# A causal convolution and a maxout feed-forward layer on one core: the second convolution bank is copied out behind the next relu, and the copy of the repacked block into the upper partitions is issued one block later, behind the x cast

## The chip, the cores and the metric

The kernel runs on one core of a Trainium2 chip. Its time is the device time of one execution in microseconds (us). Three runs of the kernel before took 529.06, 526.87 and 526.42 us; the median is 526.87 us. All data is drawn at random once and is the same in every run.

## The reference

```python
# x: 8 x 4160 x 192, weight: 8 heads x 7 taps; group = 192 / 8 = 24 channels a head
w   = softmax(weight, axis=-1)
out[b, s, h, :] = sum over k of w[h, k] * x_padded[b, s + k, h, :]    # 6 zero rows ahead of each sequence
y   = out.reshape(33280, 192)
h   = max(max(y @ w1, y @ w2), y @ w3)                               # 192 x 768 each
result = h @ w_out                                                   # 768 x 192, float32
```

The kernel uses max(a, b, c) = max(a - c, b - c, 0) + c: it multiplies y by w1 - w3 and by w2 - w3 (both in `wd`), takes relu of the first product and the maximum with the second, multiplies by w_out, and adds y @ (w3 @ w_out), whose small matrix (`m16`) it computes once at the start.

## The kernel before

**Blocks.** The 33280 tokens are cut into 65 blocks of 512 tokens. Work on a block goes through these stages, each on its own engine:

- `load_x` (SP's queue) reads the block's rows of x into a float32 tile `xf`; `cast_x` (POOL, L133) turns them into float16 (`x16`).
- `conv` (TensorE, L222) computes the convolution as 40 matmuls against a banded matrix. Heads 0 to 3 go to one PSUM bank, G0, and heads 4 to 7 to a second one, G1. ScalarE (L231) copies G0 and then G1 into the tile `ys`.
- `repack` moves `ys` to the tile `yd`, where the 192 channels lie as 3 x 64 rows, by ten small DMAs on SP's queue (L259, "pieces" below). It runs once for a group of two blocks (the first two groups have one block each). One more DMA, on POOL's queue (L260), copies partitions 0 to 63 of `yd` to partitions 64 to 127; it is called the duplicate below. It waits until all pieces have landed, and POOL does nothing else while it waits at its head.
- `l1` (L273) computes one sixth of the 768 hidden rows, here called a sub-tile: six matmuls, three into a bank of `lp` (from partitions 0 to 63 of `yd` and `wd`) and three into a bank of `lq` (from partitions 64 to 127). The two kinds use different halves of the TensorE's rows and run side by side. Then ScalarE writes r = relu(lp) (L277), and VectorE writes h = max(r, lq) (L278). `lp` and `lq` have two banks each, so a sub-tile takes the banks of the one before the last: its `lq` matmuls wait until the max of two sub-tiles earlier is done.
- `st2` (L309) multiplies h by w_out and y by `m16` into banks `po`, again with one stream on each half of the rows: 30 pairs of matmuls a block, cut into five equal slices. ScalarE copies one half of `po` (L313), VectorE adds the other (L314), and `store` (POOL's queue, L323 and L328) writes the block to memory.

**Banks.** G0, G1 and the four `po` tiles of a block rotate through four PSUM banks, so the second pair of `po` tiles of a block takes the banks that G0 and G1 of the same turn had.

**Order.** Each engine runs its instructions in the order in which the code issues them; the order is written out by hand. The main loop turns once a block. Turn t issues: the load of block t+6; the cast of block t+5; sub-tile 0 of block t; the convolution of block t+4 with both bank copies; the repack with the duplicate, where t+4 ends a group; then sub-tiles 1 to 5 of block t, each followed by one slice of `st2` of block t-1; and the store of block t-1. The last four turns (blocks 61 to 64) have no convolution left.

**Queues.** A DMA on SP's queue waits until the DMA eight places ahead of it has landed. POOL's stream holds the casts, the duplicates and the stores in one line.

Of the kernel before, what the change touches and what calls it, by code (L numbers as in the profile page):

```python
# [14 lines left out]
P = 128  # L15
# [6 lines left out]
NBLK = 512  # L22
# [4 lines left out]
def kernel(  # L27
# [12 lines left out]
    nc = tc.nc  # L40
# [6 lines left out]
    NJ = DFF // P  # L47
# [20 lines left out]
    NB = len(blocks)  # L68
    blkN = [sum(sg[2] for sg in blk) for blk in blocks]
# [29 lines left out]
    groups = [[0], [1]] + [list(range(t, min(t + 2, NB))) for t in range(2, NB, 2)]  # L99
    group_of = {t: (g, k) for g, ts in enumerate(groups) for k, t in enumerate(ts)}  # L100
    AHEAD = 4
# [3 lines left out]
    def load_x(t):  # L105
        if not 0 <= t < NB:
            return
        chunks = chunks_of[t]
        xf = xfp.tile([P, NQMAX, D], FP32, tag="xf", name=f"xf_{t}")
        parts = []  # L110
        i, n = 0, len(chunks)
        while i < n:
            k = i
            while (k + 1 < n and chunks[k][3] == P and chunks[k + 1][3] == P
                   and chunks[k + 1][1] == chunks[k][1]
                   and chunks[k + 1][2] - chunks[k][2] == CHK):
                k += 1
            (_, b0, row0, rlen0, _, _, _) = chunks[i]
            cnt = k - i + 1
            src = bass.AP(tensor=x.tensor, offset=(b0 * SEQ + row0) * D,  # L120
                          ap=[[D, rlen0], [CHK * D, cnt], [1, D]])
            nc.sync.dma_start(out=xf[0:rlen0, i:k + 1, :], in_=src)
            parts.append((rlen0, i, k + 1))
            i = k + 1
        xin[t] = [xf, None, parts]

    def cast_x(t):
        if not 0 <= t < NB:
            return
        xf, _, parts = xin[t]  # L130
        x16 = x16p.tile([P, NQMAX, D], FP16, tag="x16", name=f"x16_{t}")
        for (rl, q0, q1) in parts:
            nc.gpsimd.tensor_copy(out=x16[0:rl, q0:q1, :], in_=xf[0:rl, q0:q1, :])  # L133
        xin[t][1] = x16
# [19 lines left out]
    for k in range(KW):  # L154
        nc.vector.tensor_mul(out=taps[:, KW - 1 - k, :], in0=wexp[:, k, :], in1=wrec[:])
    nc.scalar.dma_start(
        out=bass.AP(tensor=Rd[:].tensor, offset=Rd[:].offset,
                    ap=[[BW + NHEAD, P], [1, KW * NHEAD]]),
        in_=taps[:].rearrange("p k h -> p (k h)"))
# [5 lines left out]
    HALF, NC = 64, D // 64  # L165
# [25 lines left out]
    def make_m():  # L191
        nc.scalar.copy(out=wo[:], in_=wos[:])
        for g in range(NJ // 2):
            ps = psq.tile([P, 2, D], FP32, tag="q", name=f"pt{g}")
            for k in range(2):
                js = slice(P * (2 * g + k), P * (2 * g + k + 1))
                for c in range(NC):
                    nc.tensor.transpose(ps[:, k, HALF * c:HALF * (c + 1)], w3s[0:HALF, c, js],
                                        ident[0:HALF, 0:HALF])
            nc.vector.tensor_copy(out=w3t[:, 2 * g:2 * g + 2, 0:D], in_=ps[:])  # L200
            nc.vector.tensor_copy(out=w3t[:, 2 * g:2 * g + 2, D:2 * P], in_=ps[:, :, P:D])
        for i in range(2):
            ps = psp.tile([P, D], FP32, tag="p", name=f"pm{i}")
            for j in range(NJ):
                nc.tensor.matmul(ps[:], lhsT=w3t[:, j, P * i:P * (i + 1)], rhs=wos[:, j, :],  # L205
                                 start=(j == 0), stop=(j == NJ - 1))
            nc.vector.tensor_copy(out=m16[:, i, :], in_=ps[:])


    slots, dense, hs, outs, halves = {}, {}, {}, {}, {}  # L210

    def conv(t):
        if t >= NB:
            return
        N = blkN[t]
        G = [psw.tile([P, NBLK], FP32, tag="w", name=f"G{i}_{t}") for i in range(2)]
        x16 = xin[t][1]
        for (q, b, row_lo, rlen, lo, hi, cc) in chunks_of[t]:
            for h in range(NHEAD):
                g = h % 4  # L220
                cb = GRP * h if h < NHEAD - 1 else GRP * h - 8
                nc.tensor.matmul(  # L222
                    G[h // 4][32 * g:32 * g + 32, lo:hi],
                    lhsT=x16[0:rlen, q, cb:cb + 32],
                    rhs=band[0:rlen, h, cc:cc + hi - lo],
                    start=True, stop=True, tile_position=(0, 32 * g))
        g, k = group_of[t]
        if k == 0:
            slots[g] = ysp.tile([P, 2, 2 * NBLK], FP16, tag="ys", name=f"ys_{g}")
        for i in range(2):  # L230
            nc.scalar.copy(out=slots[g][:, i, NBLK * k:NBLK * k + N], in_=G[i][:, 0:N])  # L231
        xin.pop(t)

    pieces = []
    for h in range(NHEAD):
# [7 lines left out]
    def repack(t):  # L243


        if t >= NB or t != groups[group_of[t][0]][-1]:
            return
        g, k = group_of[t]
        yd = dense[g] = ydp.tile([P, NC, 2 * NBLK], FP16, tag="yd", name=f"yd_{g}")
        w = slice(0, NBLK * (k + 1))  # L250
        if g == 0:
            qs = (nc.sync, nc.scalar, nc.gpsimd)
            todo = [(lo, p) for p in pieces for lo in (0, HALF)]
            for n, (lo, (half, s0, c, r0, rows)) in enumerate(todo):
                qs[n % 3].dma_start(out=yd[lo + r0:lo + r0 + rows, c, w],  # L255
                                    in_=slots[g][s0:s0 + rows, half, w])
            return
        for (half, s0, c, r0, rows) in pieces:
            nc.sync.dma_start(out=yd[r0:r0 + rows, c, w], in_=slots[g][s0:s0 + rows, half, w])  # L259
        nc.gpsimd.dma_start(out=yd[HALF:P, :, w], in_=yd[0:HALF, :, w])  # L260

    def l1(t, j):

# [13 lines left out]
        nc.scalar.activation(out=r[:, 0:N], in_=ps[0][:, 0:N], func=AF.Relu)  # L277
        nc.vector.tensor_max(out=hs[t][:, j, 0:N], in0=r[:, 0:N], in1=ps[1][:, 0:N])  # L278

    NU = 5  # L280

    def st2(t, u):

        if t < 0:
            return
        g, k = group_of[t]
        hT, y = hs[t], dense[g]
        if u == 0:  # L290
            todo = [[], []]
            for s in range(4):
                tok = slice(NBLK * k + P * s, NBLK * k + P * (s + 1))
                for i in range(2):
                    row = slice(HALF * i, HALF * (i + 1))
                    mm = [(y[row, i, tok], m16[row, 0, :])]
                    if s % 2 == i:
                        mm.append((y[row, 2, tok], m16[row, 1, :]))
                    mm += [(hT[row, j, P * s:P * (s + 1)], wo[row, j, :]) for j in range(NJ)]
                    todo[i] += [(s, n == 0, n == len(mm) - 1, m) for n, m in enumerate(mm)]  # L300
            halves[t] = (todo, {})
        todo, ps = halves[t]
        n = len(todo[0])
        for e in range(n * u // NU, n * (u + 1) // NU):
            for i in range(2):
                s, first, last, (a, b) = todo[i][e]
                if (s // 2, i) not in ps:
                    ps[s // 2, i] = psw.tile([P, 2, D], FP32, tag="w", name=f"po{i}_{t}_{s}")
                nc.tensor.matmul(ps[s // 2, i][:, s % 2, :], lhsT=a, rhs=b, start=first, stop=last)  # L309
            s, _, last, _ = todo[1][e]  # L310
            if last and s % 2 == 1:
                a = tp.tile([P, 2, D], FP32, tag="a", name=f"a_{t}_{s}")
                nc.scalar.copy(out=a[:], in_=ps[s // 2, 0][:])  # L313
                nc.vector.tensor_add(out=outs[t][:, s - 1:s + 1, :], in0=a[:], in1=ps[s // 2, 1][:])  # L314
# [16 lines left out]
    assert all(n == NBLK for n in blkN)  # L331
    for t in range(AHEAD):
        conv(t)
        repack(t)
        if t + 3 <= AHEAD + 1:
            load_x(t + 3)
        if t + 3 <= AHEAD:
            cast_x(t + 3)
        if t == 1:
            make_m()  # L340
    for t in range(NB):
        load_x(t + AHEAD + 2)
        cast_x(t + AHEAD + 1)
        hs[t] = hp.tile([P, NJ, NBLK], FP16, tag="h", name=f"h_{t}")
        outs[t] = outp.tile([P, 4, D], FP32, tag="o", name=f"o_{t}")
        l1(t, 0)
        conv(t + AHEAD)
        repack(t + AHEAD)
        for j in range(1, NJ):
            l1(t, j)  # L350
            st2(t - 1, j - 1)
        store(t - 1)
    for u in range(NU):
        st2(NB - 1, u)
    store(NB - 1)
# [1 line left out]
_INS = ['x', 'weight', 'moe_w1', 'moe_w2', 'moe_w3', 'moe_w_out']  # L357
# [26 lines left out]
```

## Time and profile before

| | us |
|---|---|
| Median of the runs | 526.87 (526.42 to 529.06) |
| The profiled execution's own time | 529.13 |
| Its span, from the first to the last instruction | 527.4 |
| TensorE (PE) busy | 481.8, 91% of the span |
| ScalarE (ACT) busy | 356.7, 68% |
| VectorE (DVE) busy | 336.6, 64% |
| POOL busy | 143.1, 27% |

The profile is of one execution. Times in it are microseconds from the span's start, and those of a single instruction in groups are nanoseconds. A timeline row gives an instruction's start, its length, its engine and line, the tile that it writes and those that it reads, how many were merged, and in brackets the idle time of the engine just before it and what ended this. A row of the view of waits gives an engine's line, what it waited for, the total in us, how many times, and the longest. PE's matmuls are pipelined and their ends are modelled, so the start of one to the start of the next says more than a length does.

### The profile page before, as it was taken

What the parts mean: (1) busy time and instruction counts of PE and PEld (TensorE: products, weight loads), DVE (VectorE), ACT (ScalarE), POOL (GpSimd) and SP (SyncE); (2) the same over time, 40 slices, a digit from 0 to 9 for tenths busy, and PEclk for the clock granted to TensorE, in tenths of its full rate; (3) what the DMA queues carried; (4) which work ended last, traced back from release to release, by engine and by line L of the source; (5) the groups of instructions that cost most, each with busy time, mean ns of one, the idle gap of its engine ahead of it and who ended that gap; (6) DMA issues with size and microseconds to landing.
All of it is one profiled execution on the core that took longest, in us unless ns stands there. A gap on an engine that the chain in (4) does not pass through costs nothing.

```text
span 527.4 us, 21248 instructions
## 1 busy us (share of the span) xinstructions
PE 481.8 (91%) x8906; PEld 359.9 (68%) x8906; DVE 336.6 (64%) x542; ACT 356.7 (68%) x654; POOL 143.1 (27%) x205
## 2 busy tenths in 40 slices
PE   0094999999999999999999999999999999999993
PEld 0082677777767777777777777777677777777773
DVE  1322677766667667676667776676666777676773
ACT  1133777777777777777777777777677777777662
POOL 1131133333331322333333222223333322322213
PEclk9997999999999999999999999999999999999998
DMA  7825566666655665666766656666666666654522
GB/s 178 203 78 129 141 189 190 193 189 192 194 141 161 179 175 155 192 192 193 188 185 176 163 165 166 183 168 185 187 191 188 186 171 171 177 140 128 140 70 61
DMA packets 65751, 87.72 MB, mean 166 GB/s; under 512 B 7592, under 2 KB 51304, under 8 KB 65656
## 3 DMA queue, kind: packets, MB, share of 16 engines
q1 hardware_dynamic: 54648, 47.36, 33.6%
q0 software_dynamic: 10224, 38.28, 25.3%
q8 instruction: 70, 1.15, 0.9%
q10 hardware_dynamic: 784, 0.72, 0.4%
q14 instruction: 25, 0.20, 0.1%
HBM read 34.93 MB, written 25.85 MB: 115 GB/s over the span
## 4 chain that ended last, share of the span: by engine, by line
PE 76%; DMA 8%; SPq 5%; POOL 3%; issue 3%; ACT 2%; ACTq 1%; DVE 1%; POOLq 0%
PE po L309 26%; PE lp L273 23%; PE lq L273 21%; PE G L222 6%; SPq L259 5%; DMA yd<-ys 3%; DMA Rd<-taps 2%; DMA xf<-in_x_dram 2%; POOL x L133 1%; DMA bandc<-Rd 1%; DMA Rd<-zero 1%; ACTq L255 1%; ACT r L277 1%; ACT ys L231 1%; DVE h L278 1%
## 5 line engine op out<-in xcount | busy, mean ns | idle before, releaser
L278 DVE TENSOR_TENSOR h<-r,lq 128x512 f16<-128x512 f16 x390 | 268.4, 688 | 153.7 <-ACT r L277 126.8
L273 PE MATMUL lq<-yd,wd 64*128 64x512 f16 x1170 | 316.2, 377 | 0.9 <-DVE h L278 0.7
L273 PE MATMUL lp<-yd,wd 64*128 64x512 f16 x1170 | 316.6, 378 | 0.0
L277 ACT ACTIVATE r<-lp 128x512 f16<-128x512 f32 x390 | 234.1, 600 | 109.8 <-PE lp L273 86.1
L309 PE MATMUL po<-wo,h 64*128 64x192 f16 x3120 | 230.3, 243 | 0.2 <-DVE h L278 0.2
L309 PEld LDWEIGHTS <-h 64*128 64x128 f16 x3120 | 189.8, 94 | 29.5 <-DVE h L278 0.4
L273 PEld LDWEIGHTS <-wd 64*128 64x128 f16 x2340 | 148.9, 94 | 51.5 <-issue 13.7
L309 PE MATMUL po<-m,yd 64*128 64x192 f16 x780 | 96.6, 243 | 0.0
L260 POOL DMA_DIRECT2D yd<-yd x33 | 18.1, 548 | 288.5 <-DMA xf<-in_x_dram 153.2
L231 ACT CAST ys<-G 128x512 f16<-128x512 f32 x130 | 69.8, 589 | 29.9 <-PE G L222 19.5
L222 PEld LDWEIGHTS <-x 128*32 128x32 f16 (+2 forms) x2624 | 37.0, 98 | 63.0 <-issue 38.8
L222 PE MATMUL G<-band,x 128*32 128x122 f16 (+3 forms) x2624 | 43.5, 212 | 36.2 <-DVE band L186 24.9
L133 POOL CAST x<-xf 128x960 f16<-128x960 f32 (+3 forms) x88 | 68.4, 794 | 30.0 <-DMA xf<-in_x_dram 29.2
L314 DVE TENSOR_TENSOR o<-a,po 128x384 f32<-128x384 f32 x130 | 71.2, 547 | 1.7 <-ACT a L313 1.7
L309 PEld LDWEIGHTS <-yd 64*128 64x128 f16 x780 | 58.2, 94 | 14.6
L323 POOL DMA_DIRECT2D out_dram<-o x64 | 49.1, 767 | 59.1 <-PE G L222 36.9
L313 ACT COPY a<-po 128x384 f32<-128x384 f32 x130 | 61.9, 476 | 2.0 <-PE po L309 1.9
L187 ACT COPY band<-bandc 128x536 f16<-128x536 f16 x1 | 2.6, 2569 | 17.2 <-DMA bandc<-Rd 17.2
L183 DVE TENSOR_TENSOR wd<-ws,w3s 128x768 f16<-128x768 f32 x3 | 2.7, 953 | 12.0 <-DMA w3s<-in_moe_w_dram 12.0
L205 PE MATMUL pm<-wos,w3t 128*128 128x192 f32 x24 | 6.9, 474 | 0.0
L205 PEld LDWEIGHTS pm<-wos,w3t 128*128 128x128 f32 x24 | 6.6, 298 | 0.1
L328 POOL DMA_DIRECT2D out_dram<-o x8 | 4.2, 537 | 0.8 <-DVE o L314 0.8
(20 smaller groups left out, 17.9 us busy)
## 6 DMA issues: line engine op xcount, KB each, us to landing
out_dram<-o POOLq DMA_DIRECT2D x64, 384.0 KB, 5.6
xf<-in_x_dram SPq DMA_DIRECT2D x48, 480.0 KB
yd<-yd POOLq DMA_DIRECT2D x31, 384.0 KB, 6.1
yd<-ys SPq DMA_DIRECT2D x186, 48.0 KB
xf<-in_x_dram SPq DMA_DIRECT2D x16, 384.0 KB
yd<-ys SPq DMA_DIRECT2D x62, 32.0 KB
ws<-in_moe_w_dram SPq DMA_DIRECT2D x2, 576.0 KB
w3s<-in_moe_w_dram SPq DMA_DIRECT2D x2, 576.0 KB
```

The source lines that it names most:

```text
L133: nc.gpsimd.tensor_copy(out=x16[0:rl, q0:q1, :], in_=xf[0:rl, q0:q1, :])
L222: nc.tensor.matmul(G[h // 4][32 * g:32 * g + 32, lo:hi], lhsT=x16[0:rlen, q, cb:cb + 32], rhs=band[0:rlen, h, cc:cc + hi - lo], start=True ...
L231: nc.scalar.copy(out=slots[g][:, i, NBLK * k:NBLK * k + N], in_=G[i][:, 0:N])
L259: nc.sync.dma_start(out=yd[r0:r0 + rows, c, w], in_=slots[g][s0:s0 + rows, half, w])
L260: nc.gpsimd.dma_start(out=yd[HALF:P, :, w], in_=yd[0:HALF, :, w])
L273: nc.tensor.matmul(ps[i][:, 0:N], lhsT=wd[row, c, P * j:P * (j + 1)], rhs=y[row, c, NBLK * k:NBLK * k + N], start=(c == 0), stop=(c == NC ...
L277: nc.scalar.activation(out=r[:, 0:N], in_=ps[0][:, 0:N], func=AF.Relu)
L278: nc.vector.tensor_max(out=hs[t][:, j, 0:N], in0=r[:, 0:N], in1=ps[1][:, 0:N])
L309: nc.tensor.matmul(ps[s // 2, i][:, s % 2, :], lhsT=a, rhs=b, start=first, stop=last)
L313: nc.scalar.copy(out=a[:], in_=ps[s // 2, 0][:])
L314: nc.vector.tensor_add(out=outs[t][:, s - 1:s + 1, :], in0=a[:], in1=ps[s // 2, 1][:])
L323: nc.gpsimd.dma_start(out=out[g0:g0 + n, :].rearrange("(s p) c -> p s c", p=P), in_=ob[:])
```

## The change

ScalarE's copy of the bank G1 is now issued behind the relu of sub-tile 1, and the repack follows it. The duplicate of a group becomes a function of its own, `double`, which is issued in the next turn of the loop, behind that turn's cast. In the four turns ahead of the loop it is issued behind the load and the cast of that turn. In the last four turns, which have no convolution, `st2` is cut into six slices instead of five, and its first slice comes directly behind sub-tile 0; the last block's `st2` is cut into six as well.

```diff
--- before.py
+++ after.py
@@ -207,7 +207,7 @@
             nc.vector.tensor_copy(out=m16[:, i, :], in_=ps[:])
 
 
-    slots, dense, hs, outs, halves = {}, {}, {}, {}, {}
+    slots, dense, hs, outs, halves, convs = {}, {}, {}, {}, {}, {}
 
     def conv(t):
         if t >= NB:
@@ -227,9 +227,15 @@
         g, k = group_of[t]
         if k == 0:
             slots[g] = ysp.tile([P, 2, 2 * NBLK], FP16, tag="ys", name=f"ys_{g}")
-        for i in range(2):
-            nc.scalar.copy(out=slots[g][:, i, NBLK * k:NBLK * k + N], in_=G[i][:, 0:N])
+        convs[t] = G
         xin.pop(t)
+
+    def evac(t, i):
+        if t >= NB:
+            return
+        g, k = group_of[t]
+        N = blkN[t]
+        nc.scalar.copy(out=slots[g][:, i, NBLK * k:NBLK * k + N], in_=convs[t][i][:, 0:N])
 
     pieces = []
     for h in range(NHEAD):
@@ -257,7 +263,13 @@
             return
         for (half, s0, c, r0, rows) in pieces:
             nc.sync.dma_start(out=yd[r0:r0 + rows, c, w], in_=slots[g][s0:s0 + rows, half, w])
-        nc.gpsimd.dma_start(out=yd[HALF:P, :, w], in_=yd[0:HALF, :, w])
+
+    def double(t):
+        if not 0 <= t < NB or t != groups[group_of[t][0]][-1] or group_of[t][0] == 0:
+            return
+        g, k = group_of[t]
+        w = slice(0, NBLK * (k + 1))
+        nc.gpsimd.dma_start(out=dense[g][HALF:P, :, w], in_=dense[g][0:HALF, :, w])
 
     def l1(t, j):
 
@@ -277,9 +289,7 @@
         nc.scalar.activation(out=r[:, 0:N], in_=ps[0][:, 0:N], func=AF.Relu)
         nc.vector.tensor_max(out=hs[t][:, j, 0:N], in0=r[:, 0:N], in1=ps[1][:, 0:N])
 
-    NU = 5
-
-    def st2(t, u):
+    def st2(t, u, NU):
 
 
 
@@ -331,27 +341,38 @@
     assert all(n == NBLK for n in blkN)
     for t in range(AHEAD):
         conv(t)
+        evac(t, 0)
+        evac(t, 1)
         repack(t)
         if t + 3 <= AHEAD + 1:
             load_x(t + 3)
         if t + 3 <= AHEAD:
             cast_x(t + 3)
+        double(t)
         if t == 1:
             make_m()
     for t in range(NB):
+        NU = NJ - 1 if t + AHEAD < NB else NJ
         load_x(t + AHEAD + 2)
         cast_x(t + AHEAD + 1)
+        if t > 0:
+            double(t + AHEAD - 1)
         hs[t] = hp.tile([P, NJ, NBLK], FP16, tag="h", name=f"h_{t}")
         outs[t] = outp.tile([P, 4, D], FP32, tag="o", name=f"o_{t}")
         l1(t, 0)
         conv(t + AHEAD)
-        repack(t + AHEAD)
+        evac(t + AHEAD, 0)
+        if NU == NJ:
+            st2(t - 1, 0, NU)
         for j in range(1, NJ):
             l1(t, j)
-            st2(t - 1, j - 1)
+            if j == 1:
+                evac(t + AHEAD, 1)
+                repack(t + AHEAD)
+            st2(t - 1, j - NJ + NU, NU)
         store(t - 1)
-    for u in range(NU):
-        st2(NB - 1, u)
+    for u in range(NJ):
+        st2(NB - 1, u, NJ)
     store(NB - 1)
 # ---- launch: one core; inputs and outputs as the reference has them ----
 _INS = ['x', 'weight', 'moe_w1', 'moe_w2', 'moe_w3', 'moe_w_out']
```

Two places show what moves. The first is ScalarE's order in turn 2 of the loop (r_1 is the relu of sub-tile 1, G_6_769 and G_6_770 are the banks G0 and G1 of block 6, a_1 is the first copy of `po`). Before:

```order
L231 CAST ys_811<-G_6_769 128x512
L231 CAST ys_811<-G_6_770 128x512
L277 ACTIVATE r_1_822<-lp_1_814 128x512
L277 ACTIVATE r_2_847<-lp_2_839 128x512
L277 ACTIVATE r_3_870<-lp_3_862 128x512
```

and now:

```order
L238 CAST ys_811<-G_6_769 128x512
L289 ACTIVATE r_1_821<-lp_1_813 128x512
L238 CAST ys_811<-G_6_770 128x512
L289 ACTIVATE r_2_847<-lp_2_839 128x512
L289 ACTIVATE r_3_870<-lp_3_862 128x512
```

The relu of sub-tile 1 and the copy of G1 have changed places; the rest of ScalarE's turn is as it was.

The second is POOL's stream in turns 1 to 4 (x_6 to x_9 are the casts, yd the duplicates, out_dram the stores). Before:

```order
L133 CAST x_6_553<-xf_433 128x960
L260 DMA yd_612<-yd_612 64x3072
L323 DMA out_dram<-o_438 128x4x192
L133 CAST x_7_753<-xf_550 128x768
L133 CAST x_7_753<-xf_550 94x192
L323 DMA out_dram<-o_556 128x4x192
L133 CAST x_8_942<-xf_750 128x192
L133 CAST x_8_942<-xf_750 128x768
L260 DMA yd_1002<-yd_1002 64x3072
```

and now:

```order
L133 CAST x_6_553<-xf_433 128x960
L333 DMA out_dram<-o_438 128x4x192
L133 CAST x_7_752<-xf_550 128x768
L133 CAST x_7_752<-xf_550 94x192
L272 DMA yd_623<-yd_623 64x3072
L333 DMA out_dram<-o_556 128x4x192
L133 CAST x_8_942<-xf_749 128x192
L133 CAST x_8_942<-xf_749 128x768
L333 DMA out_dram<-o_757 128x4x192
```

The duplicate has moved behind one store and one cast, and stands ahead of the next store.

## The prediction, made before the result was known

> **What bounds the kernel now.** I read the busy shares first, then the chain of waits.
>
> ```profile
> span 527.4 us, 21248 instructions
> PE 481.8 (91%) x8906; PEld 359.9 (68%) x8906; DVE 336.6 (64%) x542; ACT 356.7 (68%) x654; POOL 143.1 (27%) x205
> ...
> PE 76%; DMA 8%; SPq 5%; POOL 3%; issue 3%; ACT 2%; ACTq 1%; DVE 1%; POOLq 0%
> ```
>
> TensorE sets the end, and the rest of the chain leaves it for SP's DMAs and POOL now and then. So I ask where TensorE loses time, and list its timeline over one turn (block 28, starting at 249.56; parts left out).
>
> ```profile
> 249.56 0.38 PE L273 MATMUL lp<-yd,wd 64*128 64x512 f16 x1
> ...
> 250.00 0.38 PE L273 MATMUL lp<-yd,wd 64*128 64x512 f16 x1
> 250.16 0.38 PE L273 MATMUL lq<-yd,wd 64*128 64x512 f16 x1
> 250.47 0.65 PE L222 MATMUL G<-band,x 128*32 128x122 f16 x40
> 251.05 0.39 PE L273 MATMUL lp<-yd,wd 64*128 64x512 f16 x1
> ...
> 251.49 0.38 PE L273 MATMUL lp<-yd,wd 64*128 64x512 f16 x1
> ...
> 252.63 0.38 PE L273 MATMUL lp<-yd,wd 64*128 64x512 f16 x1
> 252.64 0.38 PE L273 MATMUL lq<-yd,wd 64*128 64x512 f16 x1
> 252.85 0.32 PE L309 MATMUL po<-wo,h 64*128 64x192 f16 x3
> ...
> 253.34 0.38 PE L273 MATMUL lp<-yd,wd 64*128 64x512 f16 x1
> 253.51 0.37 PE L273 MATMUL lq<-yd,wd 64*128 64x512 f16 x1
> ...
> 254.49 0.38 PE L273 MATMUL lp<-yd,wd 64*128 64x512 f16 x1
> ...
> 256.77 0.38 PE L273 MATMUL lp<-yd,wd 64*128 64x512 f16 x1
> ...
> 256.94 0.38 PE L273 MATMUL lq<-yd,wd 64*128 64x512 f16 x1
> ```
>
> The two streams run level in sub-tiles 1 and 2 (252.63 and 252.64). In sub-tile 3 `lq` starts 0.17 behind `lp`, and this lag is still there when the next block starts (256.77 and 256.94). The `lp` stream runs on, so PE looks busy; but the convolution uses all rows and waits for the later stream. It starts at 250.47, 0.47 behind the last `lp` matmul (250.00) and 0.31 behind the last `lq` (250.16). With no lag it starts 0.17 sooner, and everything after it too. The lag comes from here:
>
> ```profile
> 250.41 0.60 ACT L277 ACTIVATE r<-lp 128x512 f16<-128x512 f32 x1
> 251.16 1.07 ACT L231 CAST ys<-G 128x512 f16<-128x512 f32 x2 [0.16 <-PE G L222]
> 252.12 0.62 ACT L277 ACTIVATE r<-lp 128x512 f16<-128x512 f32 x1
> 253.04 0.60 ACT L277 ACTIVATE r<-lp 128x512 f16<-128x512 f32 x1 [0.30 <-PE lq L273]
> 254.19 0.60 ACT L277 ACTIVATE r<-lp 128x512 f16<-128x512 f32 x1 [0.55 <-PE lp L273]
> 254.68 0.47 ACT L313 COPY a<-po 128x384 f32<-128x384 f32 x1
> ...
> 252.77 0.69 DVE L278 TENSOR_TENSOR h<-r,lq 128x512 f16<-128x512 f16 x1 [1.04 <-ACT r L277]
> 253.67 0.69 DVE L278 TENSOR_TENSOR h<-r,lq 128x512 f16<-128x512 f16 x1 [0.21 <-ACT r L277]
> ...
> DVE h L278 <- ACT r L277: 126.8, 203, 8.0
> ```
>
> Relus start 0.41 behind the last `lp` matmul of their sub-tile (250.00 to 250.41, 252.63 to 253.04). That of sub-tile 1 would start at 251.90 (251.49 + 0.41); both bank copies stand ahead of it, and it starts at 252.12. Its max ends at 253.46 (252.77 + 0.69), and `lq` of sub-tile 3, which takes that bank, starts 0.05 later, at 253.51.
>
> TensorE's second loss is a missing cast:
>
> ```profile
> 255.74 0.54 POOL L260 DMA_DIRECT2D yd<-yd  x1 [9.74 <-DMA xf<-in_x_dram]
> 256.27 0.78 POOL L323 DMA_DIRECT2D out_dram<-o  x1
> 257.05 0.99 POOL L133 CAST x<-xf 128x960 f16<-128x960 f32 x1
> ...
> 258.10 0.65 PE L222 MATMUL G<-band,x 128*32 128x122 f16 x40 [0.36 <-POOL x L133]
> ```
>
> POOL stands 9.74 us at the duplicate; the store and the cast queue behind it, and the convolution waits for the cast.
>
> **The change part by part.** The sum is made against the profiled execution: 529.13, of which the span is 527.4 and 1.7 lies outside it.
>
> *The relu ahead of the G1 copy.* I work the turn out from its start with no lag, so all after the convolution is 0.17 earlier. `lp` of sub-tile 1 starts at 1.32 (251.05 − 249.56 − 0.17), its last at 1.76, its relu at 2.17. The G0 copy starts at 1.43 (251.16, less 0.17), and two copies of 1.07 together, 0.59 each, follow one another by 0.48, so ScalarE is free at 1.91. The relu is not held. Its max starts 0.65 later (252.12 to 252.77), at 2.82, and ends at 3.51; `lq` of sub-tile 3 may start at 3.56. `lp` of sub-tile 3 comes at 3.61 (253.34 less 0.17). The lag is gone, with 0.05 to spare. The G1 copy goes 0.49 behind the relu (as 254.19 to 254.68), at 2.66, and lets the next relu go at 3.14; that is due at 3.31 (253.04 less 0.17). Later sub-tiles have the same margin: the max of sub-tile 2 ends at 254.36 and `lq` of 4 may start at 254.41, 0.08 ahead of `lp` of 4 at 254.49. So the price is 0.17 a turn. Turns with it:
>
> ```profile
> 60.52 0.38 PE L273 MATMUL lp<-yd,wd 64*128 64x512 f16 x1
> ...
> 82.37:154.46 72.09, 72.09 (x1364) 53.71 (x1362) 50.38 (x80) 54.00 (x101) 19.18 (x26) 1.00 0.64 178
> ...
> 489.82 0.38 PE L273 MATMUL lp<-yd,wd 64*128 64x512 f16 x1
> ...
> 490.46 0.38 PE L273 MATMUL lp<-yd,wd 64*128 64x512 f16 x1
> 490.89 0.37 PE L273 MATMUL lq<-yd,wd 64*128 64x512 f16 x1
> ...
> 509.58 0.38 PE L273 MATMUL lp<-yd,wd 64*128 64x512 f16 x1
> ```
>
> Ten turns from 82.37 to 154.46 take 72.09, 7.209 each, at full granted clock (1.00), with PE busy throughout: the lag is regular. Blocks 3 to 60 begin with it: 58 × 0.17 = **−9.9**. Bounds: 0, if the wait comes back elsewhere, and 9.9, as nothing is left to take.
>
> *G1 held longer.* The bank is read until 3.25 (2.66 + 0.59) instead of 2.67 (251.16 + 1.07). The second `po` pair, which takes it, starts about 4.5, in the third slice; 1.2 to spare, so 0. SP's pieces of the second half stand behind five others; ten of them take 7.9 (the row of SP below), so the sixth starts some 4 behind the first: 0.
>
> *The duplicate behind the cast.* Blocks 2 to 60 take 489.82 − 60.52 = 429.3; 59 × 7.209 is 425.3. The 4.0 left over are waits for casts, as at 258.10. Now the cast waits only for the store, which leaves early in the turn, and for its own load, issued a turn earlier. **−4.0**; bounds 0 and 4.0. In other runs the share may be smaller: the median lies 2.3 below the profiled time.
>
> *What is late next.* The duplicate still waits for its pieces, so it should leave when it did: at 255.74, 6.18 into its turn (249.56).
>
> ```profile
> DMA to landing us min/median/max: 2.8/6.0/8.0
> 244.56 7.91 SPq L259 DMA_DIRECT2D yd<-ys  x10
> ...
> 45.29 0.99 POOL L133 CAST x<-xf 128x960 f16<-128x960 f32 x1 [1.36 <-DMA xf<-in_x_dram]
> ...
> 53.16 0.99 POOL L133 CAST x<-xf 128x960 f16<-128x960 f32 x1
> ```
>
> It lands at 6.18 + 6.0 = 12.2 and is read two turns after its own began, at 14.08 (2 × 7.04): 1.9 to spare, 0. The Trainium skill, "DMA: Bandwidth & Descriptors", section "Anatomy of one DMA — SWDGE (gpsimd) path", gives 2.0 us plus the bytes over 436 GB/s, an estimate of 2.9 us for 384 KB. By that nothing could be late; the trace does not agree, with 6.0 at the median, and the rival below goes by the trace.
>
> *The start.* The cast that the first loop convolution needs waits for its load (45.29), not for the duplicate. The first duplicate now goes behind it, at 46.3 (45.29 + 0.99), and lands near 52.3. Block 1 reads it, but its convolution waits in any case for the cast that ends at 54.15 (53.16 + 0.99); this cast stands behind the second duplicate as it did. So 0; bounds −0.3 and +1.5, for a longest landing of 8.0 and as much again. I don't count block 2 above, since the second duplicate, which it reads, leaves just ahead of that cast and may land as late as its start (60.52).
>
> *The last four turns.* Without a convolution, sub-tiles 0 and 1 adjoin, and `lq` of sub-tile 1 lags 0.43 (490.46, 490.89) for its bank. A turn takes (509.58 − 489.82) / 3 = 6.59. With a slice between them there is no such wait: six sub-tiles of 0.65 (249.56 to 250.00 and a third step of 0.21, as 252.63 to 252.85) and 30 pairs of 0.082 (0.49 for six, 252.85 to 253.34) make 6.36. 4 × 0.23 less 0.1 for a shorter last slice ahead of the final `st2`: **−0.8**, bounds 0 and −0.9.
>
> Sum: 529.13 − 9.9 − 4.0 − 0.8 = **514.4**.
>
> **The rivals.**
>
> *The cast waits stay (518.4).* The bracket at 255.74 names an x load. If the cast's own load were late, it would wait as before: 514.4 + 4.0. Against it: the cast follows the store without idle time (256.27 + 0.78 = 257.05), so its load was there.
>
> *The lag comes back (525.1).* The margin is 0.05, and the G1 copy now sits between relus 1 and 2. Were relu 2 pushed by 0.25 (0.08 of margin and 0.17), `lq` of sub-tile 4 would lag as that of 3 did: only the 4.0 remain. It has 0.17 before the copy touches it at all. The Trainium skill, "Perfetto Trace Analysis", section "Optimization Strategy", says that a gap which repeats can mean too few buffers. By that rule two `lq` banks are the fault, and the lag would stay. The trace agrees in part: the bank is what is waited for, but sub-tiles 4 and 5 find theirs free, and only the late max makes the wait.
>
> *The duplicates come too late (546, slower).* Stores now go out ahead of the duplicate, while its pieces move. Should they delay the pieces by 2 and the landing take the longest 8.0, it lands at 6.18 + 2 + 8.0 = 16.2, 2.1 late. A wait at one group gives the next its room, so 15 of 31 groups pay: 31 us, 546. It beats the gain of 14.7 at 1.0 a wait, a landing at 15.1. Against it: only the far end of the row does this, and a store no longer leaves with the duplicate.
>
> **How the numbers follow.** The forecast has 0.80, the cast waits 0.08, the lag 0.07, the late duplicates 0.05. A measurement of this kernel can tell about 0.5%, 2.6 us. The first two are faster (0.88), 525.1 is within it (0.07), 546 is slower (0.05). The range goes from 512.0 (a start and a few turns better than worked out) to 519.0, which takes in the cast waits; together they hold about 0.85 of the chance. I take 514.5.
>
> **What would show it.** Turns of 7.04; `lp` and `lq` of sub-tile 3 starting together; VectorE idle clearly less than 1.04 before the max of sub-tile 1; hardly any wait of L222 for POOL in the loop; duplicates still 5 to 6 into a turn; last turns of 6.4. Wrong would be: a lag at sub-tile 4, waits of `lq` at a block's start for a duplicate, or a turn of 7.2.

## The result and the profile after

The changed kernel takes 514.87 us at the median of four runs (514.74 to 515.73). The kernel before took 527.67 us beside it (526.42 to 529.06, four runs). The ratio is 0.976, with a 95% interval of 0.973 to 0.9791: the change makes the kernel faster by 2.1 to 2.7%. The profiled execution took 514.83 us. Its span is 513.0 us, so the span is 14.4 us shorter than that of before.

The first rows of the profile's page of the changed kernel (span, busy times), and its chain of waits by engine:

```profile
span 513.0 us, 21247 instructions
PE 470.8 (92%) x8906; PEld 322.7 (63%) x8906; DVE 335.4 (65%) x542; ACT 355.6 (69%) x654; POOL 143.4 (28%) x205
...
PE 88%; DMA 7%; ACT 1%; SPq 1%; ACTq 1%; POOL 1%; issue 0%; DVE 0%; POOLq 0%
```

TensorE has the same 8906 matmuls but counts 11.0 us less busy time. I read that as the lag that went: while one stream lagged, half the rows stood idle, and the engine counted as busy. The chain now stays on TensorE for 88% of the span instead of 76%, and SP's queue is down from 5% to 1%.

Block 28 again, from the timeline of TensorE in the changed kernel (turn from 243.88 to 250.93; parts left out):

```profile
243.88 0.38 PE L285 MATMUL lp<-yd,wd 64*128 64x512 f16 x1
243.88 0.38 PE L285 MATMUL lq<-yd,wd 64*128 64x512 f16 x1
...
244.62 0.65 PE L222 MATMUL G<-band,x 128*32 128x122 f16 x40
245.20 0.39 PE L285 MATMUL lp<-yd,wd 64*128 64x512 f16 x1
...
247.50 0.38 PE L285 MATMUL lp<-yd,wd 64*128 64x512 f16 x1
247.50 0.38 PE L285 MATMUL lq<-yd,wd 64*128 64x512 f16 x1
...
248.64 0.38 PE L285 MATMUL lp<-yd,wd 64*128 64x512 f16 x1
248.65 0.38 PE L285 MATMUL lq<-yd,wd 64*128 64x512 f16 x1
...
250.93 0.38 PE L285 MATMUL lp<-yd,wd 64*128 64x512 f16 x1
250.93 0.38 PE L285 MATMUL lq<-yd,wd 64*128 64x512 f16 x1
```

`lp` and `lq` start together in sub-tile 3 (247.50), in sub-tile 4 (248.64, 248.65) and in the next block (250.93). The convolution stands 0.74 into the turn, where it stood at 0.91. ScalarE and VectorE in the same turn:

```profile
245.32 0.59 ACT L238 CAST ys<-G 128x512 f16<-128x512 f32 x1
246.06 0.60 ACT L289 ACTIVATE r<-lp 128x512 f16<-128x512 f32 x1 [0.15 <-PE lq L285]
246.55 0.58 ACT L238 CAST ys<-G 128x512 f16<-128x512 f32 x1
247.20 0.60 ACT L289 ACTIVATE r<-lp 128x512 f16<-128x512 f32 x1
...
246.69 0.69 DVE L290 TENSOR_TENSOR h<-r,lq 128x512 f16<-128x512 f16 x1 [0.65 <-ACT r L289]
```

ScalarE now waits 0.15 for the `l1` matmuls ahead of the relu of sub-tile 1. Before, the relu stood behind a copy. VectorE idles 0.65 ahead of that max instead of 1.04.

How long ten turns take, as a row of the windows view (length, busy times of PE, PEld, DVE, ACT and POOL, granted clock, DMA share, GB/s), and where blocks 2, 61 and 64 start:

```profile
81.81:152.29 70.48, 70.48 (x1365) 47.19 (x1362) 50.35 (x80) 53.90 (x101) 20.16 (x27) 1.00 0.67 183
...
60.66 0.38 PE L285 MATMUL lp<-yd,wd 64*128 64x512 f16 x1
...
476.43 0.38 PE L285 MATMUL lp<-yd,wd 64*128 64x512 f16 x1
...
495.51 0.38 PE L285 MATMUL lp<-yd,wd 64*128 64x512 f16 x1
```

A turn lasts 7.048 instead of 7.209. Blocks 2 to 60 take 415.77 (476.43 − 60.66) instead of 429.30, so 13.53 of the 14.4 is gained there. The start costs 0.14 (60.66 against 60.52). Blocks 61 to 63 take 19.08 instead of 19.76, and block 64 with the tail 17.5 instead of 17.8 (the spans are known to 0.1); together that is 0.9 to 1.0.

TensorE's waits for casts, in the view of waits, of the kernel before and then of the changed one (what was waited for; total, times, longest):

```profile
PE G L222 <- POOL x L133: 10.8, 9, 6.4
```

```profile
PE G L222 <- POOL x L133: 7.7, 2, 6.5
```

The two that are left stand ahead of block 1 (1.16 and 6.54). From block 1 on there is none.

### The profile page after: what moved, and what is told of

It is laid out like the page before. It is cut to its first block, busy times and chain, and to the rows that moved or that the text cites. A ratio compares the mean times of both kernels' runs of the same rounds, so it can differ in the third digit from the quotient of the medians.

```text
span 513.0 us, 21247 instructions
## 1 busy us (share of the span) xinstructions
PE 470.8 (92%) x8906; PEld 322.7 (63%) x8906; DVE 335.4 (65%) x542; ACT 355.6 (69%) x654; POOL 143.4 (28%) x205
## 4 chain that ended last, share of the span: by engine, by line
PE 88%; DMA 7%; ACT 1%; SPq 1%; ACTq 1%; POOL 1%; issue 0%; DVE 0%; POOLq 0%
PE lp L285 48%; PE po L319 31%; PE G L222 7%; PE lq L285 2%; DMA xf<-in_x_dram 2%; DMA Rd<-taps 2%; DMA bandc<-Rd 1%; DMA Rd<-zero 1%; SPq L265 1%; ACTq L261 1%; POOL out_dram L338 1%; DMA yd<-ys 1%; ACT band L187 1%; ACT ys L238 0%; DVE h L290 0%
## 5 line engine op out<-in xcount | busy, mean ns | idle before, releaser
L319 PE MATMUL po<-wo,h 64*128 64x192 f16 x3120 | 204.4, 243 | 0.4 <-DVE h L290 0.4
L319 PEld LDWEIGHTS <-h 64*128 64x128 f16 x3120 | 152.0, 94 | 58.6 <-DVE h L290 0.6
L285 PEld LDWEIGHTS <-wd 64*128 64x128 f16 x2340 | 110.0, 94 | 48.8 <-issue 3.4
L333 POOL DMA_DIRECT2D out_dram<-o x64 | 49.2, 768 | 240.5 <-DVE o L324 171.2
L238 ACT CAST ys<-G 128x512 f16<-128x512 f32 x130 | 75.4, 583 | 16.4 <-DMA yd<-ys 14.3
L319 PE MATMUL po<-m,yd 64*128 64x192 f16 x780 | 84.7, 243 | 0.0
L222 PE MATMUL G<-band,x 128*32 128x122 f16 (+3 forms) x2624 | 43.5, 213 | 33.3 <-DVE band L186 24.7
L319 PEld LDWEIGHTS <-yd 64*128 64x128 f16 x780 | 47.6, 94 | 14.8
L200 DVE COPY w3t<-pt 128x384 f32<-128x384 f32 x3 | 1.7, 555 | 4.3 <-PE pt L198 4.3
```

Of the source, the lines that this page charges most:

```text
L222: nc.tensor.matmul(G[h // 4][32 * g:32 * g + 32, lo:hi], lhsT=x16[0:rlen, q, cb:cb + 32], rhs=band[0:rlen, h, cc:cc + hi - lo], start=True ...
L285: nc.tensor.matmul(ps[i][:, 0:N], lhsT=wd[row, c, P * j:P * (j + 1)], rhs=y[row, c, NBLK * k:NBLK * k + N], start=(c == 0), stop=(c == NC ...
L333: nc.gpsimd.dma_start(out=out[g0:g0 + n, :].rearrange("(s p) c -> p s c", p=P), in_=ob[:])
```

## The experiments

Each kernel was timed beside the kernel before on the same chip. The ratios are to that.

### The two parts alone

The duplicate directly behind its pieces again, and the rest as changed:

```diff
         repack(t)
+        double(t)
...
-        double(t)
...
-        if t > 0:
-            double(t + AHEAD - 1)
...
                 repack(t + AHEAD)
+                double(t + AHEAD)
```

> The changed kernel with one part undone: the duplicate stands again directly behind the pieces, ahead of the store and the cast. The relu ahead of the G1 copy and the six last slices stay. If the parts simply add up (my theory of the prediction), the turn is 7.05 and only the 4.0 of cast waits are back: 514.9 + 4.0 = 518.9. Rival: the parts help each other. A turn that is 0.16 shorter leaves the cast 0.33 less room in two turns, so more groups wait and each waits longer; from the eight groups that waited before (each 0.5 longer, 4 in all) and four that nearly did (1 in all) I work out 3.8 + 4 + 1, which gives 522 to 524, with more than eight waits of L222 for POOL in the loop.

It took 524.25 us (ratio 0.9895, 0.9819 to 0.997), where adding up gave 518.9. The profiled execution of the same kernel took 517.68, 6.6 us less than the median, and its turns were 7.046 without a lag. So the lag was gone in that execution, and yet most of the gain was not there in the other three (524.20 to 524.62). What took their time no trace shows.

Both bank copies ahead of the relu again, and the duplicate behind the cast:

```diff
         evac(t + AHEAD, 0)
+        evac(t + AHEAD, 1)
+        repack(t + AHEAD)
...
-            if j == 1:
-                evac(t + AHEAD, 1)
-                repack(t + AHEAD)
```

> The changed kernel with the other part undone: both bank copies stand again ahead of the relu of sub-tile 1. The duplicate behind the cast and the six last slices stay. Theory: turns of 7.21 with lq of sub-tile 3 lagging 0.17, and no wait of L222 for POOL in the loop: 514.9 + 58 x 0.163 = 524.4. Rival (the late duplicate or the store ahead of it costs something of its own, hidden in the sum): slower than 526.

It took 524.92 us (ratio 0.9947, 0.9924 to 0.997; ten runs). Its turns, in the row of the windows view, are those of before, with the lag; from block 1 on no cast is waited for:

```profile
82.67:154.76 72.09, 72.09 (x1365) 53.84 (x1363) 50.38 (x80) 54.00 (x101) 20.06 (x26) 1.00 0.66 177
```

To see whether the surprise of the first of these runs comes from the order of ScalarE alone, I put only the G1 copy behind the relu in the kernel before. All else stayed as it was there, the five slices too:

```diff
         conv(t + AHEAD)
-        repack(t + AHEAD)
+        evac(t + AHEAD, 0)
         for j in range(1, NJ):
             l1(t, j)
+            if j == 1:
+                evac(t + AHEAD, 1)
+                repack(t + AHEAD)
             st2(t - 1, j - 1)
```

> The kernel before with one edit: the G1 copy stands behind the first relu. The duplicate stays directly behind its pieces, and five slices stay last. Against the run with the six slices (524.25 us timed, 517.68 profiled) only the last four turns differ, by 0.24 us each, so by the theory that the two edits depend on each other (a shorter turn brings the casts nearer to the duplicate on POOL, and the cast waits grow) the timed median is 525.2, between 524.0 and 526.5. The rival is that the edits add up: 526.9 - 9.6 of lag = 517.3 to 518.9 + 0.9 = 519.8. In the profile the turns without a stall last 7.05 to 7.07 and each stall stands before the first G matmul of a turn, released by POOL; where the timed median is at 525 and the profiled time near it, these stalls sum to about 7 us or more, and where the profiled time is again some 6 us below the timed ones, the profiled run is the one that differs.

It took 521.06 us (518.84 to 523.83, four runs; ratio 0.9863, 0.9813 to 0.9913), between the two expectations. Here the profiled execution was the longest of the four, 523.83. Its row of waits for casts, and the largest of those in the loop, in block 29, on POOL and on TensorE (timelines):

```profile
PE G L222 <- POOL x L133: 15.0, 13, 6.2
```

```profile
252.92 0.54 POOL L266 DMA_DIRECT2D yd<-yd  x1 [10.17 <-DMA xf<-in_x_dram]
253.45 0.78 POOL L329 DMA_DIRECT2D out_dram<-o  x1
254.23 1.00 POOL L133 CAST x<-xf 128x960 f16<-128x960 f32 x1
...
255.28 0.65 PE L222 MATMUL G<-band,x 128*32 128x122 f16 x40 [1.28 <-POOL x L133]
```

The duplicate leaves at 252.92, the store and the cast queue behind it, and the convolution of the next turn, which began at 253.19, waits 1.28 for the cast. The turns of the loop without a wait last 7.045; blocks 2 to 60 take 8.0 us more than 59 of those. In the profile of the run with the six slices it was 2.1 us. One and the same kernel differed by 5.0 us between runs (518.84 to 523.83), the other by 6.9 (517.68 to 524.62); the changed kernel's four runs lie within 1.0. So I take the waits for casts to be of chance size; what ends POOL's waits at the duplicate is, by its rows, the landing of x loads and of pieces. Moving the duplicate removes them: in the seven profiles with the duplicate behind the cast and the start unchanged, TensorE waits for a cast twice, both times ahead of block 1, and never after.

By the medians they are also larger once the lag is gone. The medians, in us (each beside its own runs of the kernel before, whose medians lie between 527.3 and 527.7):

| | duplicate ahead of the cast | behind the cast |
|---|---|---|
| copies ahead of the relu | 527.67, five slices | 524.92, six slices |
| G1 copy behind the relu | 521.06, five slices; 524.25, six | 514.87, six; 516.53, five |

With the copies ahead of the relu, moving the duplicate and adding the slices is worth 2.75. With the G1 copy behind it, moving the duplicate is worth 4.5 (521.06 to 516.53) or 9.4 (524.25 to 514.87). That the price rises is what the medians say, and it is not shown clear of the scatter: the ratios of the two kernels with five slices, 0.9863 (0.9813 to 0.9913) and 0.9783 (0.9724 to 0.9841), overlap in their intervals, and the shortest run of the kernel with six slices and the duplicate ahead (517.68) lies 2.8 above the changed kernel. A reason can be read from rows, though no run isolates it: in the same order of POOL the convolution that needs the cast now comes 7.05 + 0.74 = 7.79 after the start of the turn in which the duplicate leaves, instead of 7.21 + 0.91 = 8.12, so 0.33 us of slack is gone at each of some 30 groups; and the pieces of the second bank can leave later in the turn. How much of the difference between 4.5 and 9.4 is chance stays open.

### Where the G1 copy may stand

Both copies behind the relu:

```diff
-        evac(t + AHEAD, 0)
...
             if j == 1:
+                evac(t + AHEAD, 0)
                 evac(t + AHEAD, 1)
```

> Both bank copies stand behind the relu of sub-tile 1. Theory (an lq stream may start 0.05 behind the max of two sub-tiles earlier, with 0.07 to spare): relu 1 starts at 2.17 of the turn as now, the copies at 2.66 and 3.14, so relu 2 is free only at 3.62 instead of 3.31, and lq of sub-tile 4 lags 0.23 to the end of the turn. Turns of 7.28, 514.9 + 58 x 0.23 = 528.3, and a few us more where the pieces, which start 1.2 later, make the duplicate late: 528 to 534. Rival (what counts is that relu 1 goes first, whatever follows): 514.9, turns of 7.05.

It took 530.11 us (ratio 1.0049, 1.0021 to 1.0077), 15 us more than the changed kernel, and its turns last 7.296. ScalarE in one turn of it (timeline, turn from 244.23):

```profile
246.60 0.60 ACT L289 ACTIVATE r<-lp 128x512 f16<-128x512 f32 x1 [0.93 <-PE lq L285]
247.09 1.07 ACT L238 CAST ys<-G 128x512 f16<-128x512 f32 x2
248.03 0.63 ACT L289 ACTIVATE r<-lp 128x512 f16<-128x512 f32 x1
```

The relu of sub-tile 2 comes 3.80 into the turn instead of 3.32, and the lag appears one sub-tile later, at 4, and is larger (0.26 at its start). So the mechanism is the one of the prediction: what counts is which relu a copy delays, and by how much. One copy fits between two relus, two don't.

The G1 copy behind the relu of sub-tile 2, and behind that of sub-tile 3:

```diff
-            if j == 1:
+            if j == 2:
```

> The copy of G1 stands behind the relu of sub-tile 2. Theory: relu 2 starts at 3.32 of the turn, the copy at 3.81 and it ends at 4.40; relu 3 is due at 4.46 and ScalarE free at 4.29, the second pair of po tiles needs the bank at 4.51. Nothing waits: 514.9 within 1, turns of 7.05. Rival (every step that the bank is held longer costs): each turn longer by up to 0.5, 530 to 545.

```diff
-            if j == 1:
+            if j == 3:
```

> The copy of G1 stands behind the relu of sub-tile 3. Theory: relu 3 starts at 4.46, the copy at 4.95 and it ends at 5.54; the second pair of po tiles, due at 4.51 in the third slice, takes this bank and waits until 5.59, 1.08 later, and both streams with it, since the matmuls are issued in order. 59 turns: 514.9 + 59 x 1.08 = 578.6. Rival (the banks of po are never short): 514.9.

Behind sub-tile 2 it makes no difference: 515.2 us (ratio 0.9759, 0.9723 to 0.9795), turns of 7.046. Behind sub-tile 3 it is far slower: 579.02 us (ratio 1.0962, 1.0903 to 1.1021), turns of 8.11. The view of waits names the reason:

```profile
PE po L319 <- ACT ys L238: 49.9, 60, 0.8
```

Every turn the second `po` pair waits for its bank. So G1 may be held through one more sub-tile, as the prediction said (1.2 to spare), but not through two. A turn is longer by 1.07, though the row shows 0.83 for each (49.9 over 60); the weight loads of the same line stand idle for 1.06 each (63.5 over 60).

### Where the duplicate may stand

The duplicate behind the store instead of behind the cast:

```diff
-        if t > 0:
-            double(t + AHEAD - 1)
...
         store(t - 1)
+        if t > 0:
+            double(t + AHEAD - 1)
```

> The duplicate stands one place further back, behind the store of its turn, which waits for an addition 1.5 into the next turn. Theory (the price of my slower rival): it leaves at 7.05 + 1.5 + 0.8 = 9.3 into its turn and lands 4 to 8 later, 6 at the middle: 15.3, while the block that reads it is due at 14.09. Each of 30 groups waits about 1.2 (0 to 3.2): 514.9 + 36 = 551, 530 to 575, with lq waiting at the start of each block that begins a group. Rival (duplicates have room enough): 514.9.

It took 538.82 us (ratio 1.0201, 1.0145 to 1.0257): slower than before, by the mechanism of the slower rival. It is 23.5 more than the changed kernel beside it (515.29, below), where I had taken 36. Waits of TensorE and its weight loads, and the landing of the DMAs into `yd`, as the views of waits and of the tile `yd` have them:

```profile
PE lq L285 <- DMA yd<-yd: 9.7, 19, 2.0
```

```profile
PEld L285: 22.6, 30
...
DMA to landing us min/median/max: 1.8/5.0/7.8
```

Weight loads wait 30 times: at each group, not at every second one. The duplicates of these groups leave 9.65 to 12.17 into their turn, 10.2 at the median, and land 5.0 later at the median; I had taken 6.0 and more. They land sooner although SP issues the pieces of the next group beside them, as the timelines of SP and POOL show:

```profile
113.85 8.16 SPq L265 DMA_DIRECT2D yd<-ys  x10
114.41 0.54 POOL L272 DMA_DIRECT2D yd<-yd  x1
```

So pieces beside it do not by themselves make the landing long. In the changed kernel it goes with the time of leaving: the seven duplicates of these 30 groups that leave within 5 us of their turn's start land 6.7 to 7.9 later, the five that leave after 7 us land 3.7 to 5.0 later. What else moves at those times was not isolated. Turns that begin with such a wait last 7.5 to 9.4.

### The last turns

The five slices again in the last four turns:

```diff
-        NU = NJ - 1 if t + AHEAD < NB else NJ
+        NU = NJ - 1
...
-    for u in range(NJ):
-        st2(NB - 1, u, NJ)
+    for u in range(NJ - 1):
+        st2(NB - 1, u, NJ - 1)
```

> The changed kernel with the last blocks' second matrix product cut into five slices again, as before. Theory: the last four turns take 6.59 instead of 6.36, with lq of sub-tile 1 lagging 0.42, and the wait ahead of the last product is 0.1 shorter or more: 514.9 + 0.8 = 515.7. Rival (no effect, the lag in these turns is hidden by the shorter end): 514.9.

It took 516.53 us (ratio 0.9783, 0.9724 to 0.9841). In its profile the last turns take 6.59 with the lag of 0.42, against 6.36 in the changed kernel: 0.23 a turn, 0.7 in three; block 64 with the tail takes 0.1 to 0.2 more. The rest of the 1.7 between the medians need not belong to them: in this profile two duplicates landed 0.18 and 0.43 late, which made two turns of the loop longer by 0.24 and 0.49.

### The changed kernel once more

> The changed kernel itself once more, beside the next three on one chip: 514.9 (514.7 to 516), turns of 7.05. Theory on duplicates: they land with little room, so a turn may be 0.1 to 0.5 longer here and there where lq waits for one at the start of a block. If the time of five last slices (516.5, 1.6 over the first measurement of the changed kernel) was partly the chip's, this run shows more than 515.5.

On another chip it took 515.29 us (ratio 0.9754, 0.9713 to 0.9795), less than the 515.5 above which I would have put a part of the five slices' time down to the chip. One turn of the loop was longer (7.39 instead of 7.05); the rows name no DMA for it, only "issue" (0.53 on the weight loads).

### Trying to shorten the start

Apart from the 24.7 for the banded matrix at the very start, the largest wait of TensorE's matmuls that is left is the one of 6.54 ahead of the first convolution of the loop. It waits for a cast, whose x load stands behind pieces on SP's queue. Three kernels were to shorten it. The first issues the loads of blocks 3 to 5 right behind the first piece of group 0:

```diff
...
+                if n == 0:
+                    for u in (3, 4, 5):
+                        load_x(u)
...
-        if t + 3 <= AHEAD + 1:
-            load_x(t + 3)
```

> The changed kernel with the loads of x blocks 3, 4 and 5 issued on the SP queue directly behind the first piece of group 0, ahead of the other pieces. Theory: the first conv of the loop waits for a cast (TensorE idle 6.5 us there) because its x load stands behind the pieces on SP; with the loads ahead that wait goes, and block 2 starts when the second duplicate has landed, which is bound by the pieces of the next group on SP, some 2 to 3 us before the 60.66 us of now: 57.5 to 58.5, so 512.5 us (511.5 to 513.5). Rival: the start is set by the duplicates alone, whose pieces now leave 3 x 0.1 us or more later; then the time is 514.9 to 516.

The second does the same, and shares the pieces of groups 1 and 2 between SP and POOL. The third only shares the pieces:

```diff
-        for (half, s0, c, r0, rows) in pieces:
-            nc.sync.dma_start(out=yd[r0:r0 + rows, c, w], in_=slots[g][s0:s0 + rows, half, w])
+        for n, (half, s0, c, r0, rows) in enumerate(pieces):
+            q = nc.gpsimd if g < 3 and n % 2 else nc.sync
+            q.dma_start(out=yd[r0:r0 + rows, c, w], in_=slots[g][s0:s0 + rows, half, w])
```

> The run with the early loads, and besides it the pieces of groups 1 and 2 go alternately to the SP and the POOL queue. Theory: the pieces' issue on one queue sets the landing of the second duplicate; on two queues it lands at about 51.5 to 53 us, block 2 starts near 53 to 55 in place of 60.66, and the time is 507.5 to 510 us. Rival: POOL's own issues and casts push each other, so that the second duplicate lands no sooner than with the early loads alone: 512 to 514 us.

> The changed kernel with one edit: the ten pieces of groups 1 and 2 go alternately to the SP and the POOL queue; the x loads stay where the change has them. Theory: the first loop convolution (46.30 in the changed kernel) waits for a cast whose load stands behind ten pieces of 0.73 us each on SP; with five of them there the load goes out some 3.6 us sooner, the convolution starts at 42 to 43, TensorE's gap there is about 3 us instead of 6.5, block 2 starts at 56 to 58 instead of 60.66, and the time is 510 to 512.5 us. Rival: as in the two runs with early loads, the next thing in the order takes over (the bank copies wait for their slots until the pieces have moved, or the cast waits on POOL behind pieces and duplicate), and the time is 514 to 517 us.

They took 520.39 us (ratio 0.9866, 0.983 to 0.9903), 517.99 (0.9821, 0.9784 to 0.9858) and 518.86 (0.9841, 0.9787 to 0.9894). All three are 3 to 5.5 us slower than the changed kernel, outside what both sides of my expectations allowed. In their profiles the loop is as it was; block 2 starts at 65.49, 64.90 and 64.47 instead of 60.66. SP's queue, as timelines show it, in the changed kernel and in the first of the three:

```profile
27.47 5.48 SPq L261 DMA_DIRECT2D yd<-ys  x7
33.28 0.38 SPq L122 DMA_DIRECT2D xf<-in_x_dram  x1
33.93 7.31 SPq L265 DMA_DIRECT2D yd<-ys  x10
41.35 1.02 SPq L122 DMA_DIRECT2D xf<-in_x_dram  x2
42.46 7.40 SPq L265 DMA_DIRECT2D yd<-ys  x10
```

```profile
28.47 4.88 SPq L122 DMA_DIRECT2D xf<-in_x_dram  x3
33.40 5.16 SPq L261 DMA_DIRECT2D yd<-ys  x6
38.66 14.62 SPq L268 DMA_DIRECT2D yd<-ys  x20
```

The row of the three loads is 4.88 long there, instead of 1.40 (0.38 + 1.02). The issues themselves take 1.50 (0.66, 0.47 and 0.37, in narrower windows); ahead of the third, SP waits for a load to land, as the view of its waits shows:

```profile
SPq L122 <- DMA xf<-in_x_dram: 3.2, 1, 3.2
```

The last piece of group 2 goes out by 53.28 instead of 49.86, 3.4 later, and the second duplicate leaves at 55.33 instead of 51.93, also 3.4 later: about the length of that wait. The cast behind it makes TensorE wait, as its timeline shows (first kernel of the three):

```profile
48.36 0.58 PE L288 MATMUL lp<-yd,wd 64*128 64x512 f16 x1 [3.63 <-ACT r L292]
...
56.90 1.05 PE L222 MATMUL G<-band,x 128*32 128x122 f16 x40 [3.29 <-POOL x L133]
```

So one pause of 6.54 was exchanged for two, of 3.63 and 3.29. The first comes from ScalarE, as the timelines of the changed kernel and of the first of the three show:

```profile
47.43 0.59 ACT L238 CAST ys<-G 128x512 f16<-128x512 f32 x1 [6.84 <-DMA yd<-ys]
```

```profile
47.23 0.59 ACT L238 CAST ys<-G 128x512 f16<-128x512 f32 x1 [4.70 <-DMA yd<-ys]
47.71 0.60 ACT L292 ACTIVATE r<-lp 128x512 f16<-128x512 f32 x1
```

The copy of the next bank waits for its slot in `ys` until pieces have left it, and a relu stands behind that copy. It starts at nearly the same time in both (47.43 and 47.23); in the changed kernel that wait lay under the pause for the cast. With the shared pieces POOL does the same: its pieces of group 2 stand behind the first duplicate, which leaves at 46.30 in the second kernel and 46.56 in the third, no sooner than the 46.18 of the changed kernel, and the second duplicate leaves at 55.11 and 54.69. In these two SP is done with the pieces of group 2 sooner than the 49.86 of the changed kernel (47.69 and 43.79), but the second duplicate then depends on POOL's pieces.

The second pause costs more than its length, too. Rows of the windows view of the first of the three, from 42 to 44 and from 56 to 58 (granted clock third from the end):

```profile
42.00:44.00 2.00, 2.00 (x11) 0.69 (x11) 0.69 (x1) 0.53 (x2) 0.00 (x0) 0.50 0.14 37
...
56.00:58.00 2.00, 1.10 (x42) 1.07 (x44) 0.00 (x0) 0.01 (x1) 1.28 (x2) 0.50 1.12 363
```

After the pause the clock is at half, where the changed kernel has 1.00 from 56 to 58, and the convolution takes 1.05 instead of 0.65. The changed kernel pays this once, behind its pause of 6.54. The first of the three pays it behind both of its pauses; from 48 to 50 its clock is 0.52. The Trainium skill, "TensorE: Matmul & The Clock Gate", section "What's actually happening", says that the array falls back to half rate after about 3.4 us of idling; the trace agrees for the pause of 6.54 (clock 0.50 from 46 to 48). But it also shows 0.50 behind the pause of 3.29, and from 42 to 44, ahead of both pauses of the first of the three, where TensorE's matmuls had waited at most 0.93 at a time since 24.63; so less idling can do it too.

None of the experiments beats the changed kernel.

## Why the prediction was right

**What bounds the kernel** was read rightly. TensorE's timeline showed a regular lag of 0.17 with the engine counted busy, and taking away its cause took 0.16 from every turn.

**The relu ahead of the G1 copy, −9.9.** The steps came out within 0.01: the max of sub-tile 1 starts 2.81 into the turn (2.82 worked out), the G1 copy 2.67 (2.66), the next relu 3.32 (3.31), `lp` and `lq` of sub-tile 3 at 3.62 (3.61). The turn is shorter by 7.209 − 7.048 = 0.161, so 59 turns give 9.5, 0.4 less than the term. The kernel with both copies behind the relu shows that the margin was read rightly as well: there the next relu comes 0.48 later, and the lag is back.

**G1 held longer, 0.** Right, and tested on both sides: one sub-tile more costs nothing, two more cost 1.07 a turn.

**The duplicate behind the cast, −4.0.** The sum against the profiled execution was right: 13.53 − 9.5 = 4.0 in blocks 2 to 60. But its size was not a property of the edit. By medians it was worth about 2 in the kernel before (2.75 with the slices, which are some 0.8 of it), and 4.5 to 9.4 once the G1 copy had moved. The prediction added two terms as if neither depended on the other. Alone, by the medians, the reordering of ScalarE gave 3.4 (with six slices) to 6.6 (with five) of the 9.9. In the profile of the latter TensorE waits for casts 13 times and 15.0 us in all, against 9 times and 10.8 before; of the long runs of the former there is no trace, and its one short run (517.68) has nearly the whole gain. So how the two terms depend on each other stays open in part. It doesn't show in the total, as both parts were made.

**What is late next, 1.9 to spare.** Right as to the result, with some luck in the margin. That the duplicates leave when they did was wrong: for blocks 4 to 62 they left 4.3 to 6.9 into their turn before, 5.2 at the median, and now 4.4 to 8.3, 6.3 at the median, where the list of signs had "still 5 to 6". The 6.18 was read from a single turn in which the duplicate left late, and so it came out near the new median. The landing takes 5.9 at the median (6.1 before), and 2.1 is to spare at the median. But a margin of medians does not cover the thinnest case, block 10:

```profile
109.74 0.54 POOL L272 DMA_DIRECT2D yd<-yd  x1 [3.27 <-DMA yd<-ys]
...
117.03 0.38 PE L285 MATMUL lp<-yd,wd 64*128 64x512 f16 x1
117.05 0.39 PE L285 MATMUL lq<-yd,wd 64*128 64x512 f16 x1
```

It leaves 6.8 into its turn (102.94), and `lq` of the group that it feeds starts 7.31 after it, 0.02 behind `lp`. In the run with five slices two came late by 0.18 and 0.43. The estimate of 2.9 us, worked out from the Trainium skill's "DMA: Bandwidth & Descriptors", section "Anatomy of one DMA — SWDGE (gpsimd) path", is below each of the 31 copies of this size in the changed kernel: 3.7 at the least.

**The start, 0.** It cost 0.14.

**The last four turns, −0.8.** 0.9 to 1.0 by the profile: 0.68 in three turns, as worked out (0.23 each), and 0.2 to 0.3 in block 64 with the tail.

**The rivals.** That the cast waits stay was wrong: from block 1 on none is left. That the lag comes back was wrong for this order; it does so with both copies behind the relu. That duplicates come too late is a mechanism that exists: it gave 538.82 with the duplicate behind the store. But there all 30 groups paid, where I had "15 of 31 groups pay": I read this as a duplicate that hangs on a store being put off with its turn, so that a wait at one group gives the next no room. Against that the landing was too pessimistic (5.0 instead of 8.0). Pieces that are late themselves, as the rival had it, were not tried.

The predicted 514.5 lies 0.4 below the measured median. Between the two profiled executions the gain is 14.3 (529.13 to 514.83), where the sum had 14.7; the 0.4 are the term of the lag. Beside the median of the kernel before (527.67) the gain is 12.8, since the execution that the sum started from was longer than any of its four timed runs (526.42 to 529.06).

## What to carry to other kernels

Where two streams share TensorE's rows, look at where both of them start, not at the busy share: a lag of a fraction of a matmul in one stream is invisible until the next matmul that uses all rows, and it is paid there every time round. A copy that nobody waits for should stand behind the instruction that TensorE waits for, as long as it fits into ScalarE's next gap; one copy fitted here and two did not. A wait that depends on when DMAs land has no fixed price: take it from several runs, don't expect it to stay when an edit shortens the loop, and test parts alone before adding them up.

## What the hardware showed that I had not expected

- The order of one queue went with the scatter of the times. With the duplicate ahead of store and cast, runs of one kernel on one chip differed by 5.0 us (518.84 to 523.83), by 6.9 (517.68 to 524.62) and, for the kernel before, by 5.2 (525.58 to 530.80, 19 runs). With it behind the cast they differed by 1.0 (514.74 to 515.73), by 0.3 (515.06 to 515.32) and, with the copies in the old order, by 2.0 (524.17 to 526.15, ten runs).
- A row of the timeline that merges the issues of several DMAs can hold a wait. The three loads of x fill 1.40 us of SP's rows in one place and 4.88 in another; 3.2 of the 4.88 are SP waiting for a load to land.
- The same duplicate of 384 KB lands 3.7 to 7.9 us after its issue in the changed kernel, from block 4 on. Those that leave early in the turn take longest, and pieces issued beside it don't explain that: with them the landing was 5.0 at the median, in the run with the duplicate behind the store.
